# Polysketch attention and an ELU feed-forward on one core: groups 0 and 1 taken pair by pair with own sum banks, and a new order of the head

## The chip, the cores and the metric

The kernel runs on one core of a Trainium2 chip. The core has five engines that work side by side, each through its own queue in order: TensorE (PE in the profile, with PEld for its weight loads), VectorE (DVE), ScalarE (ACT), GpSimd (POOL) and SyncE (SP), which here only issues DMA transfers. ACT also issues a few transfers. An engine waits for another by semaphores. PE writes its results to PSUM, eight banks of 128 partitions by 512 float32 values; DVE and ACT read them there.

The metric is the device time of one execution in microseconds (us); lower is better. The time before is the median of seven runs.

## The reference, cut to what matters

```python
def phi(x):
    a = np.einsum('rd,bhsd->bhsr', S1, x)
    b = np.einsum('rd,bhsd->bhsr', S2, x)
    return np.einsum('bhsi,bhsj->bhsij', a, b).reshape(*x.shape[:-1], r * r)
q_p, k_p = (phi(q), phi(k))
kv = np.einsum('bhsf,bhsd->bhfd', k_p, v)
z = np.sum(k_p, axis=2)
num = np.einsum('bhsf,bhfd->bhsd', q_p, kv)
den = np.einsum('bhsf,bhf->bhs', q_p, z)[..., None] + 1e-06
x = (num / den)                     # to (4352, 128)
h = x @ w_in                        # 128 -> 2048
g = np.where(h > 0.0, h, np.exp(np.minimum(h, 0.0)) - 1.0)
out = g @ w_out                     # 2048 -> 128
```

There are 4 images (batch), 4 heads, 1088 positions, head size 32, and r = 8, so that phi has 64 features. q, k and v are float32. S1, S2, w_in and w_out arrive as float64 and are turned into float32 on the chip, from their raw words.

## The kernel before, in words

**Tiles.** The 4352 rows of x are cut into 9 *groups*: groups 0 to 7 have 512 rows, group 8 has 256. The 2048 hidden columns are cut into 8 *pairs* of 128-column blocks. The main work is a row of *steps*, each one group with one pair: `mm1` (x times two blocks of w_in, into two `h` banks), the ELU (`elu_a`: on ACT a RELU of -h, L525, then an EXP, L527; `elu_d`: on DVE one operation to `gg`, L533), and `mm2` (gg times two blocks of w_out, summed in the bank `o`). Every float32 matmul appears twice in the trace. Before, the order is `seg` (L635): group 0 with pairs 0 and 1, group 1 with pairs 0 and 1, then each with pairs 2 and 3, then each with pairs 4 to 7; after that, groups 2 to 8 with all eight pairs. Between its stretches the sum of group 0 or 1 leaves the bank: `fin1` copies it to `oT` on ACT (L559) or adds it there on DVE (L555). At the end of a group, `fin1` transposes the sum on DVE (L563) and SP stores it.

**Weights.** `load_w` brings a pair's w_in or w_out in raw words, on SP. A rounding is three steps, cut up so that engines can share it: `RA` (DVE, L102), `RB` (ACT, L107) and `RC` (DVE: L115, L116, L120, and last L128 on DVE or L125 and L126 on POOL). The list `order` (L166) says which blocks a rounding takes: item 0 is w_in of pair 0, item 1 is all of pair 1, item 2 is w_out of pair 0; then, before, four halves of pairs 2 and 3, and whole pairs from there.

**Attention.** For each image: k is transposed (`transp`, DVE), `KF` makes its features on PE, `KF_out` copies them (ACT), `KO` makes the outer products (`kp`, DVE), `KA` sums k-features times v on PE in the bank `kv`, `KC` takes the sums out (`kvz`), `KZ1`, `KZ2` and `KS` prepare what the denominators (`SW`) and products (`kvS`) need. For each group: `q1` (q features and denominators, PE, then ACT), `q2` (DVE), `q4` (PE transposes of `qp`, ACT copies to `qpT`), `q5` (PE; then ACT and DVE copy halves to `xg`).

**The head.** Group 0 takes a shorter way, which does not have to know the denominators first: `q1_first`, `q2_first`, `q4_first`, and `q5_first`, which multiplies by kvz, then divides by the denominators (dn, xn on DVE), then transposes to xg.

**What sets the order.** Nothing is scheduled automatically: each engine does its instructions in the order in which the program emits them. The head is written out by hand (L593 to L631). The steps run in the loop at L693: at step n the program emits `mm1` of step n, the work that `at(n, ...)` has put there, the ELU, the work of `late(n, ...)`, and `mm2` of step n - 2. PSUM banks are given out by tag: `h` has four, `aux` two, `o` one and `kv` one. A tile that takes over a bank waits until the one before it has been read.

Of the kernel before, what the change touches and what calls it, by code (L numbers as in the profile page):

```python
# [27 lines left out]
def kernel(  # L28
# [45 lines left out]
    def load_hd(eng, x, src, b, t0, t1):  # L74
        if (x, b) not in hd:
            hd[x, b] = work.tile([P, 2, NT, D], F32, name="hd_" + x, tag="hd_" + x)
        eng.dma_start(hd[x, b][:, :, t0:t1, :],  # L77
                      src[b].rearrange("h (a c t) d -> (h a) c t d", a=32, c=2)[:, :, t0:t1, :])
# [64 lines left out]
    load_hd(nc.sync, "q", q, 0, 0, 8)  # L143
# [22 lines left out]
    order = [(0, 1, 0), (1, 1, 1), (0, 0, 1), (2, 1, 0), (3, 1, 0), (2, 0, 1), (3, 0, 1)]  # L166
    order += [(cp, 1, 1) for cp in range(4, NP)]
# [44 lines left out]
    hmask = const.tile([P, 2], F32, name="hmask")  # L212
    nc.vector.tensor_reduce(hmask[:], ident[:].rearrange("p (x j) -> p x j", x=2), axis=AX, op=ADD)

    idle = psum.tile([P, 512], F32, name="idle", tag="o", bufs=1)
# [19 lines left out]
    transp(kT, "k", 0, 0, KT)  # L235
# [26 lines left out]
    kv_ps, feats, zms, kvz, abps = {}, {}, {}, {}, {}  # L262
# [30 lines left out]
    def KA(b, gi):  # L293

        kp, rows = feats.pop((b, gi))
        n = 2 * D if b == 0 else D + 1
        if gi == 0:
            kv_ps[b] = psum.tile([P, 4, 2 * D], F32, name="kv", tag="kv", bufs=1)
        kv = kv_ps[b]
        for j, i in enumerate(KG[gi]):  # L300
            for g2 in range(2):
                for hp in range(2):
                    h = 2 * g2 + hp
                    off = (h * KT + i) * D
                    nc.tensor.matmul(kv[64 * hp:64 * hp + 64, g2, :n], kp[:rows, j, h].rearrange("p i j -> p (i j)"),  # L305
                                     _ap(vt[b][:rows, off:off + D], [[VN - off, 2], [1, D]]) if b == 0 else
                                     vt[b][:rows, h * KT + i, :],
                                     start=(i == 0 and g2 == 0), stop=(i == KT - 1),
                                     skip_group_check=True, tile_position=(0, 64 * hp))

    def KC(b):

        kv = kv_ps[b][:, :2, :D + 1]
        kvz[b] = work.tile([P, 2, 2, D + 1], F32, name="kvz", tag="kvz")
        if b == 0:
            nc.vector.tensor_mul(kvz[b][:], _ap(kv, [kv.ap[1], [0, 2], kv.ap[2]]),
                                 _ap(hmask[:], [[0, 2], [1, 2], [0, D + 1]]))
        else:
            nc.scalar.copy(kvz[b][:, :, 0], kv)
# [44 lines left out]
    def q1(g, tag="aux", small=False, b_k=None):  # L364

        n = qn[g]
        p = psum.tile([P, 512], F32, name="abwp", tag=tag, bufs=1 if tag == "kv" else 2)
        for i in range(n):
            (b, t), (b1, t1) = half_tile(g, i, 0), half_tile(g, i, 1)
            if (b1, t1) == (b, t + 1) and not small:  # L370
                nc.tensor.matmul(p[:, i * 96:i * 96 + 96], qT[b][:, t:t + 2, :].rearrange("p t s -> p (t s)"),  # L371
                                 SW[:, b].rearrange("p h x r -> p (h x r)"), skip_group_check=True)
                continue
            for u, (b, t) in enumerate(((b, t), (b1, t1))):
                nc.tensor.matmul(p[64 * u:64 * u + 64, i * 96:i * 96 + 96], qT[b][:, t, :],  # L375
                                 SW[:, b].rearrange("p h x r -> p (h x r)"),
                                 skip_group_check=True, tile_position=(0, 64 * u))
        if b_k is not None:
            KF(b_k, p)

        abw[g] = work.tile([P, H * 4, 3 * R], F32, name="abw", tag="abw", bufs=2)
        nc.scalar.copy(abw[g][:, :H * n, :].rearrange("p (h t) y -> p h t y", h=H),  # L382
                       p[:, :n * 96].rearrange("p (t h y) -> p h t y", t=n, h=H))
        if b_k is not None:
            KF_out(b_k)
# [46 lines left out]
    def q5_first():  # L432
        KC(0)
        KZ1(0)
        KS(0)
        round_w(round_c, 0)
        round_w(round_d, 0)
        KZ2(0)
        xps = []
        for tt in range(2):  # L440
            p = psum.tile([P, 512], F32, name="x0ps", tag="h", bufs=4)
            xps.append(p[:, :8 * (D + 1)].rearrange("p (m d) -> p m d", d=D + 1))
            for m in range(4):
                t, g2 = 2 * tt + m // 2, m % 2
                nc.tensor.matmul(p[:, 2 * m * (D + 1):2 * (m + 1) * (D + 1)], qpT[0][:, t, g2, :],  # L445
                                 kvz[0][:, g2].rearrange("p w d -> p (w d)"), skip_group_check=True)
        transp(qT, "q", 0, 8, NT)
# [3 lines left out]
        for tt in range(2):  # L451
            nc.vector.tensor_scalar(dn[:, tt], xps[tt][:, :, D], 1e-6, None, op0=ADD)
            nc.vector.reciprocal(dn[:, tt], dn[:, tt])
            nc.vector.tensor_mul(xn[:, tt], xps[tt][:, :, :D], _ap(dn[:, tt], [[1, 8], [0, D]]))
        round_w(round_e, 0)
        q1(1)
        for tt in range(2):
# [3 lines left out]
            (nc.scalar.copy if tt else nc.vector.tensor_copy)(xg[0][:, 256 * tt:256 * tt + 256], q[:, :256])  # L461
# [55 lines left out]

    def elu_a(g, cp, c, parts=(0, 1)):
# [21 lines left out]
    def mm2(g, cp, first, last):  # L540
        n = qn[g] * P
        if first:
            ops[g] = psum.tile([P, 512], F32, name="o", tag="o", bufs=1)
# [5 lines left out]
    oT = {}  # L549

    def fin1(g, last):
        n = qn[g] * P
        o = ops.pop(g)[:, :n]
        if g in oT:
            nc.vector.tensor_add(oT[g][:, :n], oT[g][:, :n], o)  # L555
            o = oT[g][:, :n]
        elif not last:
            oT[g] = work.tile([P, 512], F32, name="oT", tag="oT")
            nc.scalar.copy(oT[g][:, :n], o)  # L559
        if last:  # L560

            ob = work.tile([P, 4, 2, 2, D], F32, name="ob", tag="ob", bufs=2)
            nc.vector.transpose(ob[:].rearrange("p i u w d -> p (i u w) d"), o)  # L563
            rows = out.rearrange("(b w y t) (q d) -> b w q y t d", b=B, w=2, t=NT, q=4)
            oh = ob[:].rearrange("p i u w d -> p (i u) w d")
            for b, t, h, m in runs(g):
                for w in range(2):
                    for q_ in range(4):
                        nc.sync.dma_start(rows[b, w, q_, :, t:t + m, :], oh[32 * q_:32 * q_ + 32, h:h + m, w, :])


    def mm2_last(cp, first, last):
        g = NQ - 1
        if first:
            ops[g] = [psum.tile([P, P], F32, name="ol", tag=t, bufs=k) for t, k in (("o", 1), ("aux", 2))]
# [17 lines left out]
    keep_warm(1)  # L593
    transp(kT, "k", 0, KT, NT)
# [4 lines left out]
    q1_first()  # L599
    KO(0, 1)  # L600
# [4 lines left out]
    for i in range(3):  # L605
        KA(0, i)
    q4_first()
    q5_first()
    mm1(0, 0)
    RA(1)  # L610
    RB(1)
    elu_a(0, 0, 0)
    q2(1, 2)
    q4(1)
    RC(1)
    x1 = q5(1, True)
    elu_a(0, 0, 1, (0,))
    q5_out(1, x1)
    elu_a(0, 0, 1, (1,))
    mm1(0, 1)  # L620
    RA(2)
    RB(2)
    for c in range(2):
        elu_d(0, 0, c)
    for c in range(2):
        elu_a(0, 1, c)
    RC(2)
    RA(3)
    for c in range(2):
        elu_d(0, 1, c)  # L630
    RB(3)  # L631
# [3 lines left out]
    seg = [(g, r) for r in (range(0, 2), range(2, 4), range(4, NP)) for g in range(2)]  # L635
    seg += [(g, range(NP)) for g in range(2, NQ)]
    steps = [(g, cp, cp == r[0], cp == r[-1]) for g, r in seg for cp in r]
# [10 lines left out]
    for n, i in ((2, 3), (3, 4), (4, 5), (4, 6), (5, 7), (6, 8), (8, 9), (9, 10)):  # L648
# [3 lines left out]
        at(n, RC, i, i > 6)  # L652
# [5 lines left out]
    for b, (n_t, n_o) in enumerate(((5, (6, 7, 7)), (10, (13, 14, 14)), (16, (20, 20, 21))), 1):  # L658
        at(n_t, transp, kT, "k", b, 0, NT)
        if b == 1:  # L660
            at(6, KFs, b)
        for i in range(3):
            at(n_o[i], KO, b, i)
    for g in range(2, NQ):
        n = NP * (g - 1) + (g == 2)
        if g == 2:
            at(12, q1, g, "aux", True, 2)
            late(12, q2, g)
        elif g == 3:
            at(19, q1, g, "aux", True, 3)  # L670
            late(19, q2, g)
        elif g == 6:

            at(NP * (g - 1) - 2, q5, g - 1)
            at(NP * (g - 1) - 2, q1, g, "kv", True)
# [4 lines left out]
        at(n + 5, q4, g)  # L680
        if g != 5:
            at(n + 6, q5, g)
    for b, (n_a, n_z, n_q) in enumerate(((8, 10, 11), (15, 17, 18), (22, 24, 25)), 1):
# [9 lines left out]
    for n in range(N + 2):  # L693
        if 2 <= n < N:
            g, cp, first, last = steps[n]
# [3 lines left out]
        if 2 <= n < N:  # L699
            elu(g, cp, 0)  # L700
        if 2 <= n < N + 2:
            g2, cp2, first, last = steps[n - 2]
            if last and g2 < NQ - 1:
                mm2(g2, cp2, first, last)
                fin1(g2, cp2 == NP - 1)
        if 2 <= n < N:
# [3 lines left out]
        if 2 <= n < N + 2:  # L710
            if g2 == NQ - 1:
                mm2_last(cp2, first, last)
            elif not last:
                mm2(g2, cp2, first, last)
# [30 lines left out]
```

## Time and profile before

| | us |
|---|---|
| median of seven runs | 295.33 |
| lowest and highest | 294.15, 295.93 |
| all seven | 295.79, 295.33, 294.15, 295.93, 294.68, 295.81, 294.76 |
| profiled execution, time | 295.79 |
| profiled execution, span (first to last instruction) | 293.5 |
| mean granted TensorE clock | 0.994 |

The profile is of one execution. Its times count from the start of the span. Lines of the profile name the engine, the line of the kernel, the operation, and "output<-inputs"; a number after x is a count. Busy times of PE are modelled in part, since matmuls are pipelined. In the 40 slices of the page each slice is 7.3 us long; a digit is the busy share in tenths. "PEclk" is the clock that PE was granted, as a share of full speed. The chain of waits follows the work that ended last back to what released each piece of it, here read in order of time: start, duration, engine, output and line.

The waits of PE above 0.5 us are few: for the transpose of k of image 1 (2.1 us), for its own first operand (1.2), for the saved sum oT (1.0), and for v in the head (0.7).

```profile
engine line waited for: us in total, times, longest us
PE abp L273 <- DVE kT L233: 2.1, 1, 2.1
PE idle L219 <- DVE warm L146: 1.2, 1, 1.2
PE o L546 <- DVE oT L555: 1.0, 1, 1.0
PE kv L305 <- DMA v<-in_v_dram: 0.7, 1, 0.7
```

### The profile page before, as it was taken

To read this page: it belongs to the slowest core of one execution; us is meant where nothing else is said; L and a number is where in the kernel's file an instruction comes from. 1 tells how busy PE (TensorE), PEld (TensorE's weight loads), DVE (VectorE), ACT (ScalarE), POOL (GpSimd) and SP (SyncE) were. 2 spreads that over 40 slices of the span, in tenths; PEclk is the share of its full clock that TensorE was granted. 3 is DMA by queue.
4 is the path that set the end of the run, shared out by engine and by line. 5 is a ranking of instruction groups with operands and counts; after the bars stand their busy time and mean duration, and the time that the engine had idled before them with its cause. 6 is when DMAs were issued, how large, how long until landed. Compare 5 with 4: busy or idle time off the path is not lost.

```text
span 293.5 us, 3927 instructions
## 1 busy us (share of the span) xinstructions
PE 283.4 (97%) x1420; PEld 147.9 (50%) x1420; DVE 169.6 (58%) x307; ACT 187.4 (64%) x356; POOL 18.5 (6%) x46
## 2 busy tenths in 40 slices
PE   8989979999899999999999999999999999999995
PEld 5854434545464545445444544445445544444694
DVE  6899999982963567363544354454443644354442
ACT  2359857664746378566577667666765686568682
POOL 2200034630010000100000000000000000000000
PEclk9999988999999999999999999999999999999999
DMA  6999749002020200002000200010002000100020
GB/s 182 336 262 254 146 105 130 2 3 73 2 38 0 36 1 2 0 2 34 4 0 4 31 2 0 0 27 9 2 0 37 0 3 0 22 13 0 0 38 18
DMA packets 37266, 13.36 MB, mean 46 GB/s; under 512 B 31744, under 2 KB 35456, under 8 KB 37248
## 3 DMA queue, kind: packets, MB, share of 16 engines
q1 hardware_dynamic: 36608, 12.53, 19.0%
q10 hardware_dynamic: 640, 0.59, 0.7%
q8 instruction: 11, 0.18, 0.3%
q14 instruction: 7, 0.06, 0.1%
HBM read 10.88 MB, written 2.23 MB: 45 GB/s over the span
## 4 chain that ended last, share of the span: by engine, by line
PE 83%; DVE 6%; DMA 3%; SPq 3%; issue 1%; ACT 1%; DVEq 0%
PE o L546 35%; PE h L516 35%; DMA v<-in_v_dram 3%; PE kv L305 3%; PE ol L579 3%; SPq L89 2%; PE xps L494 2%; PE qtp L473 2%; DVE gg L533 1%; PE abp L273 1%; PE abwp L375 1%; PE abwp L371 1%; PE x0ps L445 1%; SPq L77 1%; DVE W L102 1%
## 5 line engine op out<-in xcount | busy, mean ns | idle before, releaser
L533 DVE SCALAR_TENSOR_TENSOR gg<-e,h 128x512 f32<-128x512 f32 (+1 forms) x144 | 92.8, 653 | 101.3 <-ACT e L527 101.0
L516 PE MATMUL h<-xg,W 128*128 128x512 f32 (+1 forms) x288 | 128.7, 570 | 0.8 <-ACT xg L461 0.5
L546 PE MATMUL o<-gg,W 128*128 128x512 f32 x256 | 123.1, 603 | 1.0 <-DVE oT L555 1.0
L525 ACT ACTIVATE e<-h 128x512 f32<-128x512 f32 (+1 forms) x144 | 81.4, 565 | 35.8 <-PE h L516 35.3
L527 ACT ACTIVATE e<-e 128x512 f32<-128x512 f32 (+1 forms) x144 | 87.3, 606 | 4.5
L516 PEld LDWEIGHTS h<-xg,W 128*128 128x128 f32 x288 | 54.0, 190 | 64.0 <-issue 55.1
L546 PEld LDWEIGHTS o<-gg,W 128*128 128x128 f32 x256 | 47.1, 192 | 51.9 <-issue 49.2
L474 ACT COPY qpT<-qtp 128x512 f32<-128x512 f32 (+1 forms) x16 | 8.2, 562 | 14.8 <-PE qtp L473 14.8
L382 ACT COPY abw<-abwp 128x384 f32<-128x384 f32 (+1 forms) x8 | 3.7, 458 | 21.0 <-PE abwp L371 10.8
L258 DVE TENSOR_TENSOR kp<-ab 128x1024 f32<-128x1024 f32 (+1 forms) x12 | 11.0, 947 | 0.8 <-ACT ab L282 0.8
L305 PE MATMUL kv<-v,kp 128*64 128x33 f32 (+3 forms) x288 | 9.7, 224 | 0.7 <-DMA v<-in_v_dram 0.7
L305 PEld LDWEIGHTS kv<-v,kp 128*64 128x64 f32 (+1 forms) x288 | 9.1, 137 | 2.5 <-issue 1.2
L505 ACT COPY xg<-xps 128x256 f32<-128x256 f32 (+1 forms) x8 | 2.9, 359 | 10.5 <-PE xps L494 10.5
L402 DVE TENSOR_TENSOR qp<-an,abw 128x1024 f32<-128x1024 f32 (+1 forms) x9 | 9.3, 1046 | 0.3
L473 PEld LDWEIGHTS qtp<-ident,qp 128*128 128x128 f32 x60 | 7.0, 140 | 4.2 <-issue 3.6
L107 ACT ACTIVATE W<-W,ebias 128x256 uint32<-128x256 uint32 (+1 forms) x11 | 6.5, 600 | 3.2 <-DVE W L102 3.2
L579 PEld LDWEIGHTS ol<-W,gg 128*128 128x128 f32 x64 | 8.0, 192 | 0.6 <-DVE ob L563 0.3
L579 PE MATMUL ol<-W,gg 128*128 128x128 f32 x64 | 8.2, 276 | 0.0
L273 PE MATMUL abp<-Sab,kT 128*64 128x64 f32 x132 | 6.1, 261 | 2.1 <-DVE kT L233 2.1
L473 PE MATMUL qtp<-ident,qp 128*128 128x128 f32 x60 | 7.9, 273 | 0.0
L273 PEld LDWEIGHTS abp<-Sab,kT 128*64 128x64 f32 x132 | 5.7, 172 | 3.5 <-issue 2.9
L125 POOL TENSOR_TENSOR raw<-raw,tiny 128x512 f32<-128x512 f32 x4 | 5.3, 1314 | 33.7 <-DVE raw L120 33.6
(88 smaller groups left out, 131.3 us busy)
## 6 DMA issues: line engine op xcount, KB each, us to landing
raw<-in_moe_w_in_dram SPq DMA_DIRECT2D x8, 256.0 KB, 6.3
raw<-in_moe_w_out_dram SPq DMA_DIRECT2D x8, 256.0 KB, 6.4
hd_k<-in_k_dram SPq DMA_DIRECT2D x3, 544.0 KB, 7.0
hd_q<-in_q_dram SPq DMA_DIRECT2D x3, 544.0 KB, 4.0
out_dram<-ob SPq DMA_DIRECT2D x40, 32.0 KB, 1.6
v<-in_v_dram SPq DMA_DIRECT2D x12, 72.0 KB, 5.1
v<-in_v_dram SPq DMA_DIRECT2D x12, 64.0 KB, 3.3
hd_k<-in_k_dram SPq DMA_DIRECT2D x1, 288.0 KB, 3.5
```

What stands on the lines that cost most here:

```text
L258: nc.vector.tensor_mul(dst, _ap(a_, list(a_.ap[1:]) + [[0, R]]), _ap(b_, [b_.ap[1], [0, R], b_.ap[2]]))
L273: nc.tensor.matmul(to[64 * u:64 * u + 64, :], kT[b][:, u * KT + i, :], Sab[:].rearrange("p h y -> p (h y)"), skip_group_check=True, tile_p ...
L305: nc.tensor.matmul(kv[64 * hp:64 * hp + 64, g2, :n], kp[:rows, j, h].rearrange("p i j -> p (i j)"), _ap(vt[b][:rows, off:off + D], [[VN - ...
L402: nc.vector.tensor_mul(qp[g][:, h], _ap(a_, list(a_.ap[1:]) + [[0, R]]), _ap(b_, [b_.ap[1], [0, R], b_.ap[2]]))
L473: nc.tensor.transpose(p[:, o:o + P], qp[g][:, r:r + 2].rearrange("p t i j -> p (t i j)"), ident[:])
L474: nc.scalar.copy(qpT[g][:, 2 * hh:2 * hh + 2, :nh, :], p[:, :2 * nh * P].rearrange("p (h m s) -> p h m s", h=2, m=nh))
L516: nc.tensor.matmul(hs[g, cp][c][:, :n], W[:, cp, c * P:c * P + P], xg[g][:, :n])
L525: nc.scalar.activation(e, hs[g, cp][c][:, :n], RELU, scale=-1.0)
L527: nc.scalar.activation(e, e, EXP, scale=-1.0)
L533: nc.vector.scalar_tensor_tensor(gs[g, cp][:, c, :n], es[g, cp][:, c, :n], -1.0, hs[g, cp][c][:, :n], op0=ADD, op1=MAX)
L546: nc.tensor.matmul(ops[g][:, :n], W[:, cp, (2 + c) * P:(3 + c) * P], gg[:, c, :n], start=(first and c == 0), stop=(last and c == 1))
L579: nc.tensor.matmul(ops[g][i][:], gg[:, c, i * P:i * P + P], W[:, cp, (2 + c) * P:(3 + c) * P], start=(first and c == 0), stop=(last and c ...
```

## The change

Groups 0 and 1: pairs 0 and 1 still come first for each group; from pair 2 on each pair is used for group 0 and at once for group 1. Groups with even and odd numbers have sum banks of their own (tags `o0` and `o1`), so that both sums stay in PSUM; `oT` is gone. The bank `kv` is gone too: the k-v sums of images 0, 2 and 3, and one q product, use `o1`, those of image 1 a bank of `aux`. `order` has whole pairs from pair 2 on. The steps at which work is placed are set anew.

Head: the first part of q is loaded in two halves, on SP and on ACT. The transpose of the first half of k is emitted behind the making of `Sab`. The 1e-6 of group 0's denominators is put in its PSUM banks by a one-row matmul (`x0_eps`), on which the products are then summed. `kvz` of image 0 is zeroed beforehand, and its sums are copied by ACT. Pair 1 is rounded ahead of `q2` of group 1, `mm1` of step (0, 1) comes ahead of group 1's `q4`, and group 0's first `mm1` goes in halves of 256 rows.

The diff, cut to its core:

```diff
-    def load_hd(eng, x, src, b, t0, t1):
+    def load_hd(eng, x, src, b, t0, t1, c=slice(0, 2)):
...
-    load_hd(nc.sync, "q", q, 0, 0, 8)
+    load_hd(nc.sync, "q", q, 0, 0, 8, slice(0, 1))
+    load_hd(nc.scalar, "q", q, 0, 0, 8, slice(1, 2))
...
-    order = [(0, 1, 0), (1, 1, 1), (0, 0, 1), (2, 1, 0), (3, 1, 0), (2, 0, 1), (3, 0, 1)]
-    order += [(cp, 1, 1) for cp in range(4, NP)]
+    order = [(0, 1, 0), (1, 1, 1), (0, 0, 1)] + [(cp, 1, 1) for cp in range(2, NP)]
...
+    kvz = {0: work.tile([P, 2, 2, D + 1], F32, name="kvz", tag="kvz")}
+    nc.gpsimd.memset(kvz[0][:], 0.0)
+    eps = const.tile([1, 8, D + 1], F32, name="eps")
...
-    transp(kT, "k", 0, 0, KT)
...
-            kv_ps[b] = psum.tile([P, 4, 2 * D], F32, name="kv", tag="kv", bufs=1)
+            kv_ps[b] = psum.tile([P, 4, 2 * D], F32, name="kv", **(dict(tag="aux") if b == 1 else dict(tag="o1", bufs=1)))
...
         if b == 0:
-            nc.vector.tensor_mul(kvz[b][:], _ap(kv, [kv.ap[1], [0, 2], kv.ap[2]]),
-                                 _ap(hmask[:], [[0, 2], [1, 2], [0, D + 1]]))
+            for hp in range(2):
+                r = slice(64 * hp, 64 * hp + 64)
+                nc.scalar.copy(kvz[0][r, :, hp, :], kv[r])
...
+    def x0_eps():
+        xps = []
+        for tt in range(2):
+            p = psum.tile([P, 512], F32, name="x0ps", tag="h", bufs=4)
+            nc.tensor.matmul(p[:, :8 * (D + 1)], some[:1, :P], eps[:].rearrange("p m d -> p (m d)"),
+                             start=True, stop=False, skip_group_check=True)
+            xps.append(p)
+        return xps
+
+    def q5_first(xps):
+        round_w(round_c, 0)
+        round_w(round_d, 0)
+        transp(qT, "q", 0, 8, NT)
+        RA(1)
+        KZ2(0)
+        RB(1)
...
-            nc.vector.tensor_scalar(dn[:, tt], xps[tt][:, :, D], 1e-6, None, op0=ADD)
-            nc.vector.reciprocal(dn[:, tt], dn[:, tt])
+            nc.vector.reciprocal(dn[:, tt], x[:, :, D])
...
-            (nc.scalar.copy if tt else nc.vector.tensor_copy)(xg[0][:, 256 * tt:256 * tt + 256], q[:, :256])
+            nc.scalar.copy(xg[0][:, 256 * tt:256 * tt + 256], q[:, :256])
+            if tt == 0:
+                q1(1)
...
+    def mm1_first():
+        hs[0, 0] = [psum.tile([P, 512], F32, name="h", tag="h", bufs=4) for c in range(2)]
+        for tt in range(2):
+            for c in range(2):
+                s = slice(256 * tt, 256 * tt + 256)
+                nc.tensor.matmul(hs[0, 0][c][:, s], W[:, 0, c * P:c * P + P], xg[0][:, s], skip_group_check=True)
...
-            ops[g] = psum.tile([P, 512], F32, name="o", tag="o", bufs=1)
+            ops[g] = psum.tile([P, 512], F32, name="o", tag=f"o{g % 2}", bufs=1)
...
-        if g in oT:
-            nc.vector.tensor_add(oT[g][:, :n], oT[g][:, :n], o)
-            o = oT[g][:, :n]
-        elif not last:
-            oT[g] = work.tile([P, 512], F32, name="oT", tag="oT")
-            nc.scalar.copy(oT[g][:, :n], o)
...
-    q5_first()
-    mm1(0, 0)
-    RA(1)
-    RB(1)
-    elu_a(0, 0, 0)
+    q5_first(x0)
+    mm1_first()
+    RC(1)
+    for c in range(2):
+        elu_a(0, 0, c)
+    mm1(0, 1)
     q2(1, 2)
+    for c in range(2):
+        elu_d(0, 0, c)
     q4(1)
-    RC(1)
-    x1 = q5(1, True)
-    elu_a(0, 0, 1, (0,))
-    q5_out(1, x1)
-    elu_a(0, 0, 1, (1,))
-    mm1(0, 1)
     RA(2)
     RB(2)
-    for c in range(2):
-        elu_d(0, 0, c)
-    for c in range(2):
-        elu_a(0, 1, c)
+    elu_a(0, 1, 0)
+    q5(1)
+    elu_a(0, 1, 1)
     RC(2)
-    RA(3)
     for c in range(2):
         elu_d(0, 1, c)
+    RA(3)
     RB(3)
...
-    seg = [(g, r) for r in (range(0, 2), range(2, 4), range(4, NP)) for g in range(2)]
-    seg += [(g, range(NP)) for g in range(2, NQ)]
-    steps = [(g, cp, cp == r[0], cp == r[-1]) for g, r in seg for cp in r]
+    steps = [(0, 0), (0, 1), (1, 0), (1, 1)] + [(g, cp) for cp in range(2, NP) for g in range(2)]
+    steps += [(g, cp) for g in range(2, NQ) for cp in range(NP)]
...
-    for n, i in ((2, 3), (3, 4), (4, 5), (4, 6), (5, 7), (6, 8), (8, 9), (9, 10)):
+    for i in range(3, NP + 1):
+        n = 2 * i - 4
         if i > 3:
             at(n - 1, RA, i)
             late(n - 1, RB, i)
-        at(n, RC, i, i > 6)
+        at(n, RC, i, i > 4)
...
-    for b, (n_t, n_o) in enumerate(((5, (6, 7, 7)), (10, (13, 14, 14)), (16, (20, 20, 21))), 1):
+    for b, (n_t, n_o) in enumerate(((3, (5, 7, 7)), (11, (13, 15, 15)), (17, (20, 20, 21))), 1):
         at(n_t, transp, kT, "k", b, 0, NT)
         if b == 1:
-            at(6, KFs, b)
+            at(5, KFs, b)
...
-    for b, (n_a, n_z, n_q) in enumerate(((8, 10, 11), (15, 17, 18), (22, 24, 25)), 1):
+    for b, (n_a, n_z, n_q) in enumerate(((8, 10, 9), (19, 20, 21), (22, 24, 25)), 1):
         for i in range(3):
             at(n_a, KA, b, i)
```

## The prediction

> **What bounds the kernel now.** I read the page's busy shares and slices first, then the gaps of TensorE (PE), then the granted clock around them, then the chain of waits of the head.
>
> ```profile
> PE 283.4 (97%) x1420; PEld 147.9 (50%) x1420; DVE 169.6 (58%) x307; ACT 187.4 (64%) x356; POOL 18.5 (6%) x46
> ...
> PE   8989979999899999999999999999999999999995
> ...
> PEclk9999988999999999999999999999999999999999
> ```
>
> PE is the bound: after the first quarter every slice is full. The change neither adds nor removes an mm1 or mm2 matmul; a pair of steps (mm1 1.72 us, mm2 1.72 us in the chain) costs the same in any order. So it can only gain or lose where PE stands idle or runs at half clock, and past 82 us it does neither (the stretches from 82 to 266 us are all PE). Slices 6 and 7 have the lower clock. Stretches of 3.41 us around them show why:
>
> ```profile
> core 0: us, PE busy (x) PEld busy (x) DVE busy (x) ACT busy (x) POOL busy (x), PEclk, DMA share, GB/s
> ...
> 39.14:42.56 3.42, 1.36 (x19) 0.56 (x19) 3.35 (x7) 2.37 (x5) 1.97 (x2) 1.00 0.01 4
> 42.56:45.97 3.41, 3.41 (x28) 2.26 (x25) 3.34 (x6) 2.20 (x6) 1.44 (x2) 0.50 0.92 213
> 45.97:49.38 3.41, 3.41 (x9) 1.48 (x9) 3.22 (x5) 2.40 (x5) 2.25 (x2) 1.00 1.29 112
> ```
>
> A stretch in which PE is busy for 1.36 of 3.42 us is followed by one at clock 0.50. What emptied it, in the chain of waits:
>
> ```profile
> 40.72 1.23 DVE kT L233
> 41.95 0.14 issue
> 42.09 1.77 PE abp L273 x34
> 43.85 2.98 PE o L546 x4
> ```
>
> VectorE (DVE) reaches the transpose of the k of image 1 only at 40.72, behind five half-size weight roundings; PE waits 2.06 us for it (the row of PE's waits says the same), and the next four mm2 passes then take 2.98 us where 1.72 is normal. The third loss, in the timeline (start, duration, then what it waited for):
>
> ```profile
> 77.98 0.68 DVE L533 SCALAR_TENSOR_TENSOR gg<-e,h 128x512 f32<-128x512 f32 x1
> 78.58 0.68 DVE L555 TENSOR_TENSOR oT<-oT,o 128x512 f32<-128x512 f32 x1
> ...
> 79.31 1.12 PE L546 MATMUL o<-gg,W 128*128 128x512 f32 x2 [1.04 <-DVE oT L555]
> ```
>
> The single output bank is not free until DVE, late in its queue, has added it to the saved sum. Last, the head:
>
> ```profile
> 2.56 7.02 DMA v<-in_v_dram
> ...
> 13.45 2.01 PE x0ps L445 x16
> ...
> 15.92 0.42 DVE xn L454
> ...
> 18.63 1.29 DVE qp L402 x2
> ...
> 21.75 0.72 DVE W L128
> ```
>
> From v's landing at 9.58 a single thread runs to L128 at 21.75, behind which mm1(0,1) starts at 22.52 and mm1(1,0) directly after, at 24.24. From mm1(1,0) on the PE order of the two kernels is the same kind of alternation, so the start of mm1(1,0) is the mark to compare.
>
> **The change, part by part, against the profiled execution** (295.79 us, span 293.5).
>
> 1. *Pair by pair (steps).* Before, groups 0 and 1 each use two pairs, stop, save the sum and resume; now each pair serves both groups before the next. A new pair is wanted every 6.9 us of PE work (two steps of 3.43) where 3.43 was the pace. For two steps DVE then owes four gg (0.60 apart, 2.4), and one full rounding (L102 0.34, L115 0.71, L116 0.46, L120 0.61, L128 0.61: 2.7), 5.1 of 6.9 us. The transpose of k of image 1 moves from step 5 to 3. I laid DVE out with these durations from 25 us: weights of pair 2 are ready at about 30.3 (PE wants them at 31.7), the transpose ends near 32.9 and its matmuls come at 36.9. So the **2.06 us** wait goes, with 4 us in hand, and with it the half clock: 3.41 us at 0.50 costs at most **1.7 us**, and the chain has 1.26 of that in the mm2 row (2.98 - 1.72) and the rest in the 34 small matmuls.
> 2. *A bank for each group (o0, o1).* No saved sum: two ACT copies (L559, 0.58) and four DVE adds (L555, 0.68) go, which PE does not feel except at 79.31: **1.04 us**. The k-v sums of images 0, 2, 3 and one q product now live in o1. Image 2's sums are written at step 19, group 1 is transposed out at step 17; image 3's at step 22, group 3 begins to write at step 26. Nobody meets. Image 1's take one of two aux banks in steps 8 to 10, where nothing else takes one. If a meeting did occur it would cost like 79.31, about 1 us. Step 19 now issues the k-v matmuls (2.34) besides q and k features (1.74): that is PE work moved, not added, and DVE, which does gg for it at 96 to 98 us, has 4 us before mm1(21) needs the h banks.
> 3. *Front of the head.* q is split over SP and ACT. Issuing took 0.61 and 0.65 each, so ACT's v goes from 2.05 to about 2.7 and its table load to about 3.5, still ahead of its copy at 5.35. The Trainium skill (Trainium Kernel Development and Optimization, Key Constraints) says that queues of different engines share the same 16 DMA engines and that spreading only saves issue time: by the rule, nothing is gained. The row: DVE waited 0.31 us for q at 6.49. By the row 0.3 us could be had, but the new order makes DVE ready for q only at 6.27 anyway (Sab first at 4.75, then the k transposes of 0.70 each), and what follows is ACT's copy of k features, which starts about 0.1 later than 7.56. I take **+0.1**; ends: -0.2 (v, balanced over queues, lands before 9.58, but kp and qp hold the end at 12.1) and +0.6 (v on ACT is late by its issue).
> 4. *x0.* The 1e-6 now comes by two one-row matmuls before v has landed, under PE's 0.68 us wait there; the two DVE adds (0.20 apart) go. kvz is two ACT copies (the similar L319 row: 0.19 each) at 12.25, before ACT's qpT copy at 12.80: hidden. Recip waits for x0ps at 14.59 as the add did. Ahead of it in DVE's queue now stand RA(1) (0.34) and SW (0.11), which end at 14.37: hidden by 0.2. xn's second half ends at 16.23 (16.34 before). mm1(0,0) in halves starts at 16.84, finishes at **18.6** where it finished at 19.55: PE gains 1.0 there.
> 5. *Second pair first.* DVE then does RC(1) before q2(1). From 16.2: RC(1) 2.5 -> 18.7; q2(1) 2.55 (1.34 and 2 x 0.60) -> 21.25; two gg 1.2 -> 22.45; RA(2) 0.2 -> 22.65. ACT: RB(2), which waits for RA(2), 0.4 -> 23.2; then, behind it in ACT's queue, elu_a(0,1,0) 1.17 -> 24.4, then the xg copy 0.37 -> 24.75. PE: mm1(0,1) 18.9 to 20.6, qtp to 21.85, q5(1) 22.7 to 23.3, then nothing until xg: mm1(1,0) at about **24.85** where it was 24.24: **+0.6**. The gain of part 4 is lost because group 1's xg comes last in this order, behind a rounding step and an ELU.
>
> Sum: 295.79 - 2.06 - 1.7 - 1.04 + 0.6 + 0.1 = **291.7 us**, if the clock stays whole.
>
> **The clock in the new gap.** Between 20.6 and 24.85 PE is idle for about 2.7 of 4.2 us. The Trainium skill (TensorE: Matmul & The Clock Gate, "What's actually happening" and the oscillation part) has the clock halved after an idle window of about 3.4 us, windows running freely, and warns of idle gaps over 3.4 us: by it neither kernel has such a gap, nothing is charged, and the answer is 291.7. The trace does not agree: 2.06 us idle in a row, 60% of one stretch, was enough, while the stretch 18.66 to 22.08 with 3.09 busy kept its clock. By the row, a 3.4 us stretch with some 1.8 us idle trips it. In the new gap, starts from 20.7 to 22.5 do, 1.8 of 3.4: about half of the executions pay 1.7 us, 293.4. The seven runs of before look like such a coin: 294.15, 294.68, 294.76, then 295.33 to 295.93, about 1.2 apart, and the profiled one, with its half clock, is of the upper four. A median over runs lies between the two values: I forecast **292.5 us**, 2.8 below the median of 295.33 (which is itself of the upper bunch, so the sum holds for it too, less 0.5).
>
> **Rivals.**
> - *The gap closes* (ACT or DVE is quicker than laid out, or PE's order fits better): mm1(1,0) at about 23, no half clock: 291.7 - 1.9 = 289.8. Against it: every duration in part 5 is from a row and the queues are in order. 0.12.
> - *The stall only moves*: weights of pair 2 late as those of pair 1 now are. RB(3) on ACT waits for RA(3) on DVE, which stands behind a gg that waits for ACT (about 1 us idle on both). If that and the POOL roundings (L115 once took 1.71 beside them, not 0.68) push pair 2 or the k transpose 3 us past my layout, PE waits about 1.5 and pays a second half clock: 292.5 + 1.5 + 1.0 = 295.0, no measurable change. Against: 1.4 us margin on pair 2, 4 on k. 0.11.
> - *Slower: RA(1) holds up x0.* It now stands in DVE's queue ahead of the first recip and waits for both transfers of pair 1, issued at 4.48 and 5.4, with 4.0 to 7.2 us to landing: by 13.1 at the latest by those numbers; RA(1) would start at 13.92. The trace proves only that they had landed by 16.96. Each us past 14.1 is a us on the end. At 16.96 it is 2.9, and the clock is lost too: 293.4 + 2.9 = 296.3, slower; it decides from there. 0.06.
> - *The forecast*, own range 291.3 to 293.8: 0.71.
>
> **How the numbers follow.** A measurement tells about 0.3% (0.9 us) from no change. The range takes the forecast's own ends with part 3's -0.2 and +0.6 and the gap's error, and reaches towards the first two rivals: 290.3 to 294.3. Faster (below 294.4): forecast, first rival and a little of the second, 0.86; same 0.08; slower 0.06.
>
> **What would show it.** Right: no wait of PE on the k transpose, no oT rows, no gap at the start of group 2; mm1(0,0) done near 18.6, mm1(1,0) at 24.5 to 25.2 released by ACT's xg copy; at most one stretch at 0.50, if any right after 25. Wrong: mm1(1,0) before 24 or after 26, a new PE wait after 26 us on DVE or POOL, or x0's recip released by a weight rounding.

## The result, and the profile after

| | before, us | changed, us |
|---|---|---|
| median | 294.85 (60 runs) | 292.23 (23 runs) |
| lowest to highest | 293.92 to 296.54 | 290.97 to 295.17 |
| profiled execution, time | 295.79 | 292.19 |
| its span | 293.5 | 290.4 |

The ratio of the times is 0.9913, 95% interval 0.9895 to 0.9932: the changed kernel is faster, by 0.9%. Its times fall into three groups: eleven from 290.97 to 291.87, six from 292.23 to 292.77, and six from 294.62 to 295.17. The granted clock, on record for each of these runs and for the profiled one, tells the first two groups apart: 0.997 to 1.000 in all eleven, 0.994 in all six and in the profiled execution. One stretch of 3.41 us at half clock takes 0.006 from the mean over 290 us. Of the third group four runs have 1.000 and two (295.17 both) 0.994.

The page of the changed kernel, first the span, then PE and its clock in 40 slices:

```profile
span 290.4 us, 3936 instructions
...
PE   7998999999999999999999999999999999999994
...
PEclk9997999999999999999999999999999999999999
```

The two slices of lower clock at 37 to 51 us are gone; there is one at 22 to 29 us. The waits of PE, longest first:

```profile
engine line waited for: us in total, times, longest us
PE h L529 <- DVE raw L116: 1.2, 1, 1.2
PE idle L223 <- DVE warm L147: 1.2, 1, 1.2
PE abp L276 <- DVE kT L237: 0.5, 2, 0.3
```

The wait of 2.1 us for the k transpose of image 1 and that of 1.0 us for oT are gone; the 0.5 here belongs to image 0, in the head. One wait is new, in front of an mm1 (L529). The name in that row misleads: DVE's L116 began at 24.28 and ended by chance just before. ACT and PE's weight load around that moment, in the timeline, show the true releaser:

```profile
23.02 0.58 ACT L545 ACTIVATE e<-h 128x512 f32<-128x512 f32 x1
23.63 0.63 ACT L547 ACTIVATE e<-e 128x512 f32<-128x512 f32 x1
24.17 0.35 ACT L518 COPY xg<-xps 128x256 f32<-128x256 f32 x1
...
24.57 0.30 PEld L529 LDWEIGHTS h<-xg,W 128*128 128x128 f32 x2 [1.68 <-ACT xg L518]
```

mm1(1,0) waits for the xg copy of group 1, and this stands in ACT's queue behind the ELU of step (0, 1). What follows is seen in stretches of 3.41 us (columns as in the prediction; the clock is the third number from the end):

```profile
21.74:25.15 3.41, 2.04 (x20) 0.68 (x19) 2.39 (x8) 3.29 (x8) 0.00 (x0) 1.00 0.64 96
25.15:28.57 3.42, 3.42 (x6) 1.36 (x5) 2.60 (x6) 2.01 (x4) 0.00 (x0) 0.50 0.91 292
```

This execution paid a half clock behind the new gap, as the profiled one before paid one behind the old gap.

### The profile page after: what moved, and what is told of

Same layout as the page of the kernel before. It is cut to its first block, busy times and chain, and to the rows that moved or that the text cites. A ratio compares the mean times of both kernels' runs of the same rounds, so it can differ in the third digit from the quotient of the medians.

```text
span 290.4 us, 3936 instructions
## 1 busy us (share of the span) xinstructions
PE 282.8 (97%) x1428; PEld 147.7 (51%) x1428; DVE 165.5 (57%) x288; ACT 186.9 (64%) x355; POOL 17.0 (6%) x49
## 4 chain that ended last, share of the span: by engine, by line
PE 94%; DVE 2%; DMA 2%; issue 0%; ACTq 0%; ACT 0%
PE h L529 40%; PE o L566 39%; PE kv L309 3%; PE ol L589 2%; PE xps L507 2%; PE qtp L486 2%; DMA hd_k<-in_k_dram 2%; PE abp L276 1%; PE abwp L380 1%; PE abwp L376 1%; PE x0ps L441 0%; PE x0ps L456 0%; DVE W L128 0%; PE qtp L434 0%; DVE W L115 0%; DVE xn L465 0%
## 5 line engine op out<-in xcount | busy, mean ns | idle before, releaser
L529 PE MATMUL h<-xg,W 128*128 128x512 f32 (+1 forms) x284 | 128.1, 574 | 1.3 <-DVE raw L116 1.2
L529 PEld LDWEIGHTS h<-xg,W 128*128 128x128 f32 x284 | 53.7, 191 | 63.6 <-issue 56.4
L261 DVE TENSOR_TENSOR kp<-ab 128x1024 f32<-128x1024 f32 (+1 forms) x12 | 12.1, 1040 | 1.7 <-ACT ab L285 1.7
L107 ACT ACTIVATE W<-W,ebias 128x512 uint32<-128x512 uint32 (+1 forms) x9 | 6.0, 666 | 3.2 <-DVE W L102 3.1
L507 PE MATMUL xps<-qpT,kvS 64*32 64x256 f32 (+2 forms) x176 | 6.8, 316 | 0.2 <-ACT qpT L487 0.2
L125 POOL TENSOR_TENSOR raw<-raw,tiny 128x512 f32<-128x512 f32 x4 | 4.2, 1043 | 44.5 <-DMA v<-in_v_dram 31.2
L507 PEld LDWEIGHTS xps<-qpT,kvS 64*32 64x32 f32 x176 | 3.2, 105 | 6.1 <-ACT e L547 5.3
```

What stands on the lines that cost most here:

```text
L261: nc.vector.tensor_mul(dst, _ap(a_, list(a_.ap[1:]) + [[0, R]]), _ap(b_, [b_.ap[1], [0, R], b_.ap[2]]))
L507: nc.tensor.matmul(xp[w][D * h:D * h + D, :nh * P].rearrange("p (m s) -> p m s", s=P)[:, m0:m0 + m, s], kvS[64 * w:64 * w + 64, b, h, :], ...
L529: nc.tensor.matmul(hs[g, cp][c][:, :n], W[:, cp, c * P:c * P + P], xg[g][:, :n])
```

## The experiments

"To the last matmul" below is the time from the start of mm1(1,0) to the start of PE's last matmul in a profile. It leaves out the head and the end, which is 5.9 to 6.1 us from the last matmul to the measured time in all these profiles. Some kernels are given by the groups of their times as well as by ratio, since a median of six runs depends on how many fell in which group. The ratios are to runs of the kernel before that were taken together with those of each kernel.

**The steps without the new head.** Order of steps, banks and roundings of the change, behind the old head:

```diff
-    seg = [(g, r) for r in (range(0, 2), range(2, 4), range(4, NP)) for g in range(2)]
+    steps = [(0, 0), (0, 1), (1, 0), (1, 1)] + [(g, cp) for cp in range(2, NP) for g in range(2)]
...
     q5_first()
     mm1(0, 0)
     RA(1)
```

> The steps, banks and roundings of the change behind the head of the kernel before. My theory (the steps bring the whole gain, the new head gives a little back because group 1's xg comes late and leaves PE idle): mm1(1,0) at 24.2 as before, no wait of PE on the k transpose, no half clock at 25, time about 291.0 us, at or below the changed kernel's 292.2. Rival (the new head carries part of the gain): 292.8 or more, with new PE waits on weights of pair 2 behind 24 us.

Measured: 290.55 (290.43 to 291.28, 4 runs), ratio 0.9846 (0.9819 to 0.9873). So the steps bring the whole gain and more, and the new head as a whole costs 1.7 us in the median (2.0 by the ratios; four runs). The waits of PE in its profile have none for the k transpose, oT, or a late xg of group 1:

```profile
PE idle L218 <- DVE warm L146: 1.2, 1, 1.2
PE sps L248 <- DVE Sx L229: 0.6, 1, 0.6
PE h L515 <- ACT xg L460: 0.5, 1, 0.5
PE h L515 <- DVE W L128: 0.4, 1, 0.4
```

To the last matmul it takes 259.85 us (25.31 to 285.16).

**Two banks alone, on the kernel before.**

```diff
-            ops[g] = psum.tile([P, 512], F32, name="o", tag="o", bufs=1)
+            ops[g] = psum.tile([P, 512], F32, name="o", tag=f"o{g % 2}", bufs=1)
...
-    steps = [(g, cp, cp == r[0], cp == r[-1]) for g, r in seg for cp in r]
+    steps = [(g, cp, cp == 0, cp == NP - 1) for g, r in seg for cp in r]
...
-            oT[g] = work.tile([P, 512], F32, name="oT", tag="oT")
-            nc.scalar.copy(oT[g][:, :n], o)
```

> The kernel before with two output banks alone: sums of groups 0 and 1 stay in PSUM between their stretches, oT is gone, the k-v sums go to o1, aux and o0; order of steps, roundings and head as before. Theory: only the 1.04 us wait at 79.31 goes; the 2.06 us wait for the k transpose and the half clock stay: 1.0 lower in each group of times, 293.1 and 294.8, median near 294.2. Rival: freeing DVE of four adds and ACT of two copies also shortens the wait at 42 us: 293 or less in the median.

Measured: 292.17 (five of 292.16 to 292.32, one of 294.29), ratio 0.9901 (0.9872 to 0.9930). The rival was right: more than the one wait goes. In the chain the transpose starts 0.5 us earlier, and the wait in front of KF is 1.6 us instead of 2.1:

```profile
40.24 1.24 DVE kT L233
41.48 0.14 issue
41.61 1.23 PE abp L273 x34
42.85 1.91 PE o L546 x4
```

KF took 1.23 here and mm2 1.91, so this execution had no half clock, and none of the six runs has a granted clock below 0.998. What moved the transpose stands at 31 to 34 us. In the kernel before, ACT waits 0.74 us for PE to finish the sum, copies it to oT, and only then starts the next ELU, for which DVE waits:

```profile
31.41 0.59 ACT L559 COPY oT<-o 128x512 f32<-128x512 f32 x1 [0.74 <-PE o L546]
31.89 0.60 ACT L525 ACTIVATE e<-h 128x512 f32<-128x512 f32 x1
...
33.19 0.69 DVE L533 SCALAR_TENSOR_TENSOR gg<-e,h 128x512 f32<-128x512 f32 x1 [0.41 <-ACT e L527]
```

With two banks that ELU starts 1.3 us earlier, and both `gg` run without a wait:

```profile
30.60 0.58 ACT L525 ACTIVATE e<-h 128x512 f32<-128x512 f32 x1
...
32.12 1.28 DVE L533 SCALAR_TENSOR_TENSOR gg<-e,h 128x512 f32<-128x512 f32 x2
```

To the last matmul: 261.78 (24.28 to 286.06).

**Is the half clock the cause of the two groups before?** Four spare matmuls in PE's wait for the k transpose, which change no result:

```diff
+        for i in range(4):
+            nc.tensor.matmul(f[:, :256], some[:, :P], some[:, :256], skip_group_check=True)
...
+            at(6, fill)
             at(6, KFs, b)
```

> The kernel before with four spare matmuls of 256 columns (0.43 us each) in PE's wait for the k transpose of image 1, in a bank that is free then; nothing else moves. Clock theory: the wait stays, the half clock after it goes, and the upper group of times (295.3 to 296.5, about half of them) moves to the lower one (293.9 to 294.9): median 294.2 to 294.4. Rival (the two groups have another cause, such as the moment at which the clock first rises): the same split.

Measured: 294.40 (22 runs), ratio 0.9963 (0.9945 to 0.9981). Three of its 22 runs are above 295.2; of the kernel before, measured beside it, 19 of 27 were. By the granted clock (0.994 or less) 17 of those 27 had the half clock and 1 of these 22, at 296.55. The few other runs above 295.2, two of each kernel, kept their clock (0.997 or more); what made them long is not traced. PE in the timeline:

```profile
39.93 1.89 PE L656 MATMUL fill<-some 128*128 128x256 f32 x8
42.19 1.24 PE L273 MATMUL abp<-Sab,kT 128*64 128x64 f32 x34 [0.37 <-DVE kT L233]
43.35 1.98 PE L546 MATMUL o<-gg,W 128*128 128x512 f32 x4
```

KF starts at the same moment (42.09 before), and all behind it runs at full clock. To the last matmul: 263.85 (24.31 to 288.16) against 265.41 (24.24 to 289.65) in the profile before: the half clock cost 1.56 us.

This kernel and the one with two banks alone both ran at full clock, so their difference of 2.07 us can be read matmul by matmul: 0.55 at the k wait, 1.31 at the wait for oT (1.20 before its first mm2 and 0.11 behind it), and 0.21 near the end, where the first sum of group 8 shares the one bank `o` with group 7 and waits for its transposition. First one bank, then two:

```profile
275.93 0.72 DVE L563 STREAM_TRANSPOSE ob<-o 128x512 f32<-128x512 f32 x1 [0.86 <-PE o L546]
276.71 0.97 PEld L579 LDWEIGHTS ol<-W,gg 128*128 128x128 f32 x8 [0.35 <-DVE ob L563]
```

```profile
274.05 0.72 DVE L553 STREAM_TRANSPOSE ob<-o 128x512 f32<-128x512 f32 x1 [0.86 <-PE o L546]
274.50 1.08 PEld L569 LDWEIGHTS ol<-W,gg 128*128 128x128 f32 x8
```

**The transpose earlier, alone, on the kernel before.**

```diff
-    for b, (n_t, n_o) in enumerate(((5, (6, 7, 7)), (10,
+    for b, (n_t, n_o) in enumerate(((3, (6, 7, 7)), (10,
```

> The kernel before with one number changed: the transpose of k of image 1 at step 3 instead of 5. If the 2.06 us wait of PE comes only from where that transpose stands in DVE's queue, the wait and the half clock after it go: 292 to 292.5 us. If it comes from the pace of the weights (DVE is busy 20.7 of 21.8 us from 24 to 46), DVE is late elsewhere by the same time and PE waits for a weight or a gg instead: 294 to 295, and the wait shows under another name.

Measured: 294.56 (22 runs), ratio 0.9979 (0.9965 to 0.9993). The wait only moved, as the rival had it:

```profile
PE o L546 <- DVE oT L555: 1.7, 2, 1.0
...
PE h L516 <- DVE gg L533: 0.5, 1, 0.5
```

To the last matmul 264.02 us (24.74 to 288.76), no better than 263.85. What is left of a gain, 0.2%, is the half clock: none of its 22 runs has a granted clock below 0.998, while 15 of the 27 of the kernel before, measured beside it, have 0.994 or less. Several short waits did not bring it on. DVE's pace, not the place of one instruction, was the limit.

**Group 1's xg first**, in the changed kernel:

```diff
     q4(1)
+    q5(1)
     RA(2)
     RB(2)
     elu_a(0, 1, 0)
-    q5(1)
     elu_a(0, 1, 1)
```

> The changed kernel with group 1's q5 and its xg copies ahead of the rounding and the ELU of step (0, 1) in the head. My theory (ACT's queue order makes xg late): mm1(1,0) at about 23.9 instead of 24.57, idle time before it 0.5 instead of 1.2 us, so the stretch of half clock becomes rare: lowest times near 290.4, median about 290.7. Rival (the ELU of step (0, 1), now later, is awaited next): mm1(1,0) early, but PE waits for gg(0,1) or the second pair and the time stays at 292.

Measured: 291.77 (291.54 to 292.15, 5 runs), ratio 0.9882 (0.9859 to 0.9906): no half clock in any of the five (0.997 or more), but not 290.7. mm1(1,0) starts at 24.60, not 23.9; the k-v sums of this execution started at 10.21 instead of 9.66, and the idle time before mm1(1,0) is 0.68 instead of 1.20. The ELU and the rounding that were moved back are now waited for, by mm2(0,0) and by an mm1 (1.2 us of idle PE together, by the starts of its matmuls; 260.98 us to the last matmul):

```profile
26.97 1.99 PE L566 MATMUL o<-gg,W 128*128 128x512 f32 x4 [0.42 <-DVE W L128]
...
32.59 1.98 PE L529 MATMUL h<-xg,W 128*128 128x512 f32 x4 [0.21 <-DVE gg L553]
```

**The new gap filled**, in the changed kernel, with three spare matmuls that change no result:

```diff
     q4(1)
+    keep_warm(1, 128)
...
     q5(1)
+    keep_warm(2)
```

> The changed kernel with three spare matmuls (1 of 128 columns between q4 and q5, 2 of 256 columns after q5 of group 1) in the new gap of PE, which change no result and nothing on other engines. Clock theory: mm1(1,0) stays at 24.6, the stretch at clock 0.50 after 25 us goes, the times of 292.2 to 292.8 move to 291.0 to 291.5. Rival (the half clock does not come from the idle time, or the split of the times has another cause): the same split of times as in the changed kernel. Times of 294.6 and above, of which the changed kernel has 6 in 23, have a cause I do not know yet; if they are a late warm-up of the clock in the first 16 us, they stay.

Measured: 290.45, 290.49, 290.97, 291.19, 291.60 and 294.70, ratio 0.9875 (0.9833 to 0.9917). No time lies in the middle group and no granted clock is below 0.998, as the clock theory wants; six runs are few. The profile fell on the 294.70, and its chain shows what an execution with a time of the third group looks like. First the changed kernel, then this one:

```profile
8.50 1.08 PE x0ps L441 x4
9.58 0.08 issue
9.66 2.46 PE kv L309 x72
12.12 1.02 PE qtp L434 x8
```

```profile
9.60 2.05 PE x0ps L441 x4
11.65 4.24 PE kv L309 x72
15.89 1.75 PE qtp L434 x8
```

The same matmuls take up to twice as long: PE's clock is still at half at 16 us. The first clock event in this trace, a rise, comes at 17.35 us; in the other profiles it comes between 4.05 and 11.71. The one-row matmuls of the 1e-6 then stand ahead of the k-v sums, and mm1(1,0) starts at 28.80 instead of 24.57.

**The 1e-6 matmuls left out or widened.** Without them (the 1e-6 added on DVE as before), and with 128 rows instead of one (127 of them zero):

```diff
-            nc.tensor.matmul(p[:, :8 * (D + 1)], some[:1, :P], eps[:].rearrange("p m d -> p (m d)"),
-                             start=True, stop=False, skip_group_check=True)
```

```diff
-            nc.tensor.matmul(p[:, :8 * (D + 1)], some[:1, :P], eps[:].rearrange("p m d -> p (m d)"),
+            nc.tensor.matmul(p[:, :8 * (D + 1)], some[:, :P], eps[:].rearrange("p m d -> p (m d)"),
```

> The changed kernel without the two one-row matmuls that put 1e-6 into the banks of x0; the 1e-6 is added on DVE again, as in the kernel before. Theory: in the executions at 294.6 and above the PE clock stays at half until about 17 us, and the one-row matmuls, 2.05 us long then, stand ahead of the k-v sums, which could start at 9.7 and start at 11.6. Without them the late group of times goes down by about 2, to 292.5 to 293.2, while the lowest times stay near 291.0 or rise by up to 0.2 (the DVE adds). Rival (the matmuls keep PE awake and the clock rises earlier with them): the late group stays, and is more frequent.

> The changed kernel with the two matmuls that put 1e-6 into the banks of x0 reading 128 rows (row 0 as before, the others zero) instead of one; same result, same columns. Theory of the late times: in an execution whose clock stretch ends while the one-row matmuls run, that work hardly counts as activity, the clock stays at half for one or two stretches more, and everything in the head takes twice its time (rise at 17.35 us in the profile with spare matmuls, against 4.7 to 11.7 elsewhere). With 128 rows the rise comes at 12 us at the latest and no time lies above 293. Rival (the number of rows does not matter): about one time in four at 294.6 or above, as in the changed kernel.

Measured without: 290.98 to 291.11 (four) and 292.56, 292.60. With 128 rows: 290.51 to 292.86 (six). The ratios are 0.9877 (0.9850 to 0.9905) and 0.9879 (0.9847 to 0.9910). Neither has a time above 293, nor has either of the two mixed heads below that lack the one-row matmuls. Together that is 0 of 23 runs, where kernels with them have 7 of 45 at 294.6 or above. It points to the one-row matmuls, but does not settle it: the kernel before has none of them, and 2 of its 27 runs measured beside these kernels were at 297.88 and 298.37, 3.6 us and more above its lowest. Kernels without them also have runs 2 us above their lowest at full granted clock: 292.25 in the mixed head without them, below, and 294.29 with two banks alone.

**A mixed head**: the changed kernel up to the first mm1, from there the order of the old head; with the one-row matmuls, without, and with 128 rows:

```diff
     mm1_first()
-    RC(1)
-    for c in range(2):
-        elu_a(0, 0, c)
-    mm1(0, 1)
+    elu_a(0, 0, 0)
     q2(1, 2)
+    q4(1)
+    RC(1)
+    x1 = q5(1, True)
```

> The changed kernel up to the first mm1 in halves, and from there the order of the head before: q2 of group 1 ahead of the rounding of pair 1, group 1's xg between the two halves of the ELU of step (0, 0), then mm1(0, 1). Theory: the first part of the new head gives 1.0 us, the second part takes it back, so together mm1(0, 1) is at about 21.2 and mm1(1, 0) at 22.9 instead of 24.57: lowest times near 289.5. Rival (pair 0's w_out rounding or gg(0,0) then holds up mm2(0,0)): mm1(1, 0) early, but PE waits at 24 to 26 us and the lowest times are at 290.5 as with the head before.

> The same without the one-row matmuls (the 1e-6 added on DVE). Theory: lowest times as in the mixed kernel or 0.2 above, no times 3.4 us above the lowest, at most 2 above. Rival: as for the changed kernel without them.

> The kernel of mixed head (changed kernel up to the first mm1, then the order of the head before) with the 1e-6 matmuls of 128 rows. Theory as for the changed kernel with 128 rows: lowest times 290.5, no time above 292.5. Rival: a late group near 294.

| | median | lowest to highest | ratio |
|---|---|---|---|
| one row | 291.20 | 290.53 to 291.38 | 0.9858 (0.9833 to 0.9883) |
| none | 290.57 | 290.36 to 292.54 | 0.9863 (0.9832 to 0.9894) |
| 128 rows | 290.85 | 290.46 to 291.25 | 0.9845 (0.9820 to 0.9870) |

These beat the changed kernel and equal the old head with the new steps; none reached 289.5. The hoped-for gain of 1.0 from the early mm1(0,0) is not there. DVE in the profile of the first:

```profile
16.19 0.42 DVE L465 TENSOR_TENSOR xn<-x0ps,dn 128x256 f32<-128x256 f32 x1
17.68 0.29 DVE L396 TENSOR_TENSOR pw<-abw 128x128 f32<-128x128 f32 x1 [1.06 <-ACT abw L387]
...
20.23 0.69 DVE L115 SCALAR_TENSOR_TENSOR W<-raw,W 128x512 uint32<-128x512 uint32 x1
...
22.15 0.73 DVE L128 SCALAR_TENSOR_TENSOR W<-raw,W 128x512 f32<-128x512 f32 x1
```

DVE waits 1.06 us for group 1's q product, which the new head puts behind x0's transpose, then does q2 and the rounding, and mm1(0,1) comes at 22.94, no earlier than the 22.52 before (the k-v sums started 0.46 later in this execution, at 10.17). An early mm1(0,0) is worth nothing here: DVE's queue sets mm1(0,1), and mm1(1,0) follows at 24.66.

**q on one queue**, in the changed kernel:

```diff
-    load_hd(nc.sync, "q", q, 0, 0, 8, slice(0, 1))
-    load_hd(nc.scalar, "q", q, 0, 0, 8, slice(1, 2))
+    load_hd(nc.sync, "q", q, 0, 0, 8)
```

> The changed kernel with the first part of q loaded as before, whole and on SP. In the changed kernel DVE waited 0.42 us for q at 6.95 and PE's first k features came at 6.58 (6.39 before), behind k's second half on ACT's queue. Theory: the split does nothing for the end, since v's landing near 9.6 sets the start of the k-v sums in both: within 0.2 us of the changed kernel in each group of times. Rival (two queues bring q and v earlier): 0.3 to 0.6 slower.

Measured: 291.37, 291.76, and four of 292.59 to 292.92, ratio 0.9902 (0.9874 to 0.9930). The middle of each group lies about 0.3 above that of the changed kernel. DVE's wait for q ends at 7.15 here, and at 6.95, 6.90 and 6.51 in three profiles with two queues (the changed kernel, without the 1e-6, with 128 rows). mm1(1,0) is at 24.95; part of that can be the one-row matmuls, which ran from 8.90 to 10.04 here, ahead of the k-v sums. This leans to the rival, but six runs do not tell 0.3 us from nothing: inconclusive.

## Why the prediction was right

The time was forecast at 292.5 and came at 292.23. By its steps:

- **PE bounds the kernel, only its idle time and its clock count: right.** With the new steps and no half clock after the mark, seven profiles with the old, the changed and the mixed head take 259.8 to 259.9 us to the last matmul. Where PE idles after the mark it shows: 260.98 with group 1's xg first.
- **Part 1, the k wait and its half clock: right, and the reason too.** The pace of DVE was the cause; moving the transpose alone did nothing. In the changed kernel pair 2's weights were ready at 30.4 and the transpose at 33.2, where 30.3 and 32.9 were laid out. The half clock cost 1.56 where 1.7 was put.
- **Part 2, the banks: right in direction, too small in size.** It priced only the wait at 79.31, 1.04 us. The banks alone are worth 2.07 (263.85 less 261.78): 1.31 at that place, 0.55 at the k wait, and 0.21 where group 8 no longer waits for group 7's bank. The last two were put at nothing. The statement that PE does not feel the oT copies was the error: one of them held up ACT's ELU, and through it DVE and the transpose. No meeting of tenants in o1 or aux was seen.
- **Sum of parts 1 and 2 at full clock: 3.1 forecast, 4.0 measured** (263.85 less 259.85): 2.07 for the banks, 1.93 for the rest of the steps.
- **Part 3: open.** q was waited for 0.42 us at 6.95, more than before, and the copy of the k features (7.30) was not late. With q on one queue the groups lie 0.3 higher, so +0.1 may even have the wrong sign.
- **Part 4: mm1(0,0) early, right; hidden 1e-6, half right.** With an early clock the one-row matmuls fill PE's wait exactly (8.50 to 9.58, sums at 9.66). In the late execution they push the sums from about 9.6, when PE had done the features, to 11.65: they take 2.05 there, and the wait of 0.68 was shorter than that. In two profiles between, the sums start at 10.0 and 10.2 behind them; but they start at 9.98 and 10.17 too in the profiles without them and with 128 rows, so no cost is shown there.
- **Part 5: right.** mm1(1,0) forecast at 24.85, measured 24.57, released by ACT's xg copy as said; 24.24 before. The consequence is larger than the +0.6: with the half clock and the late starts, the new head costs 1.7 us in the median, and 0.7 without them (the first group's middle, 291.22, against 290.55).
- **The coin: right in kind, its working wrong.** A half clock came in 9 of the 24 executions whose clock is on record, near the half that was forecast. But PE was idle in the gap for 1.43 us (20.60 to 24.57), not 2.7, and at most 1.4 us of any stretch were idle. The rule taken from the row before, some 1.8 us idle in 3.4, would have charged nothing. That the share came out is luck.
- **Its two values: 291.7 and 293.4 forecast; the groups' middles are 291.22 and 292.42.** The first is lower because the banks gave more. The distance is 1.2, though the half clock itself cost 1.70 in the profile (261.55 to the last matmul, less 259.85). An estimate from 259.85 and the 6.1 us behind the last matmul puts mm1(1,0) near 25.3 in the first group, later than in the profile; the reason is not traced.
- **The third group was not foreseen.** It lifts the median: without it the other 17 runs have 291.47. The closeness of 292.5 owes something to errors that cancel: the banks' extra gain on one side, the late starts on the other.

The rivals: the gap did not close. The stall did not move to pair 2. RA(1) did not hold up x0: it ran from 13.47 and was done when x0's first recip started at 14.53, released by PE.

## What to carry to other kernels

When one engine is full, ask for each edit whether it removes that engine's idle time, and test the parts apart: here the order of the steps and a second sum bank gained 4 us at full clock, while a re-ordered head that finished its first matmul earlier lost some of it, because the next engine's queue, not that matmul, set the date. Work put into a wait to be hidden must be shorter than the wait in every execution, not only in the profiled one. Look at all the times, not only at the median: groups of times pointed to the clock, the granted clock of each run confirmed it, and a few spare matmuls in the gap showed the cause. A wait's row is not the whole price of what causes it: the copy to oT also lengthened a wait of PE 10 us later, through ACT's ELU and DVE's queue.

## What the runs showed of the hardware that was not expected

- A stretch that is in part busy can be followed by a stretch of 3.41 us at half clock: 1.36 of 3.42 us were busy in the kernel before, 2.04 of 3.41 in the changed one. The Trainium skill (TensorE: Matmul & The Clock Gate, "What's actually happening") asks for a whole idle window; the measurement decides.
- The share of busy time does not settle it either: with two banks alone, a stretch with less busy time than the changed kernel's 2.04 kept its clock, as the two lines below show. In the changed kernel 1.26 of the 2.04 us are q products on 64 rows and 32 columns (`xps`). Whether such matmuls count for less is not tested.

```profile
39.39:42.80 3.41, 1.80 (x37) 1.15 (x35) 3.41 (x6) 1.29 (x2) 2.40 (x2) 1.00 0.22 45
42.80:46.22 3.42, 3.42 (x9) 1.60 (x9) 3.35 (x6) 3.36 (x8) 1.72 (x1) 1.00 1.01 222
```

- The clock changes on a grid: in each trace the time from the first rise to the fall in the gap is a whole number of stretches of 3.41 us (8.42 to 42.56 is ten, 4.67 to 25.15 six, 8.30 to 25.37 five, the last with q on one queue). The grid lies differently in each execution, and so the same gap is cut differently: without the 1e-6 matmuls the same 1.20 us wait fell into a stretch with 2.20 us busy (23.17 to 26.58), and the clock held.
- The clock row reads full speed in the first slices even where it was not: in the late execution the k-v sums took 4.24 us instead of 2.46 there, with the row at 1.00. In the head, lengths of known matmuls tell the clock.
